# One base tile and three neighbour steps per chunk, in place of two base tiles and one step

## The chip, the cores and the metric

The kernel runs on one core of a Trainium2 chip. The metric is the device time of one execution in microseconds (us). Each kernel was run several times, in turn with the kernel before on the same chip. A run counts as slow when it lies over 1.5% above the fastest of the same kernel. Medians are over all runs of a kernel.

The engines are named as the profile names them: PE (TensorE matmul), PEld (its weight load), DVE (VectorE), ACT (ScalarE), POOL (GpSimd), SP (SyncE, which issues most of the DMAs here). A q behind a name is that engine's sequencer, which hands out its instructions. PSUM is the memory that the matmuls write.

## The reference, cut to what matters

Set attention with 32 inducing points over four batches of 12480 tokens, then a feed-forward layer on every token:

```python
# x: 4 x 12480 x 128, inducing: 32 x 128, w_in: 128 x 2048, w_out: 2048 x 128
h = mab(I, x)            # softmax over the tokens: 32 rows of 128 per batch
y = mab(x, h)            # softmax over the 32 rows: one row of 128 per token
u = y @ w_in
out = (u * clip(u + 3, 0, 6) / 6) @ w_out
```

## The kernel before

A batch is 25 chunks of up to 512 tokens. Four chunks are a group; six groups are full, the seventh has one short chunk of 192 tokens. While a batch's output is made, the next batch is loaded and aggregated (the `h` above), so the run has a start, three middle stages that do both, and a last stage that only makes output.

For the quadratic part of the feed-forward layer the kernel needs exponentials of sums of score rows: 4 tiles of 128 features per token. It does not compute them all with their own matmul. Two *base* tiles are made by a matmul and an exponential each. A *neighbour step* `d` is the exponential of a difference of score rows; it has only 32 rows, and is shared by four features each. Base times step, on DVE, gives two further tiles. The step of four chunks is made by four 32-column matmuls side by side (a *pack*; the four take 0.23 us together in the trace before), which leaves chunk j's 32 rows on partitions 32j to 32j+31 of `dk`. A DMA then spreads each row over four partitions of `d`.

```python
dpk: bufs=2   dp: bufs=4   tf: bufs=LEAD + 1   td: bufs=LEAD   osp: bufs=2   # buffers in SBUF
psF: bufs=5                                                                # PSUM banks, shared

def b_pack(b, g):                    # one per group of four chunks
    pp = psF.tile([P, 512], FP32, name="pp", tag="fb")
    for j in range(J):
        nc.tensor.matmul(pp[32 * j : 32 * j + 32, :w], lhsT=st["Wd"][:, :],
            rhs=st["xT"][:, t0 + j * w : t0 + (j + 1) * w], tile_position=(0, 32 * j))
    t = dpk.tile([P, 512], BF16, name="dk")
    nc.scalar.activation(t[: 32 * J, :w], pp[: 32 * J, :w], ACT.Exp, scale=scale)

def b_spread(b, c):                  # one per chunk, on the SP queue
    d = dp.tile([P, 512], BF16, name="d")
    nc.sync.dma_start(d[:, :w],
        st[("dk", g)][32 * j : 32 * j + 32, :w].unsqueeze(1).to_broadcast([32, 4, w]))

def b_base(b, c, k):                 # two per chunk, k = 0, 1
    nc.tensor.matmul(bp[:, :w], lhsT=st["W"][:, k]..., rhs=st["xT"][:, c0 : c0 + w])
    nc.scalar.activation(st[("x", c)][:, k, :w], bp[:, :w], ACT.Exp, scale=scale)

def b_prod(b, c):                    # one per chunk
    u = td.tile([P, 2, 512], BF16, name="TD")
    nc.vector.tensor_mul(u[:, :, :w], t[:, :, :w], d[:, :w].unsqueeze(1).to_broadcast([P, 2, w]))
    st[("T", c)] = [t[:, 0], u[:, 0], u[:, 1], t[:, 1]]
# ... 16 matmuls of 128 columns a chunk (b_quad) and one of 512 (b_lin) make its output `op`;
# DVE divides it into `os` (b_evac), and every four chunks 1 MB leaves on the SP queue

for t in range(total):               # cut: the work of the next batch goes in between
    b_evac(t - 1); b_spread(t + 4); b_prod(t + 1); b_base(t + 2, 0)
    b_lin(t); b_quad(t, 0); b_quad(t, 1); # b_pack of the group that begins at t + LEAD + 3
    b_base(t + 2, 1); b_quad(t, 2); b_quad(t, 3)
```

## Time and profile before

| | before |
|---|---|
| median of 3 runs | 324.52 us (322.81 to 328.84) |
| span of the profiled run | 319.7 us |
| PE, DVE, ACT busy | 94%, 75%, 72% |
| spread: size, from issue to landing | 128 KB, 4.1 us |

The share of busy time is read first, then by stage; the prediction below shows both. Here are the chain that ended last (by engine and by line), the largest output group and the row of the SP queue (packets, MB, share of the time of 16 DMA engines).

```profile
PE 86%; DVE 5%; ACT 3%; DMA 2%; issue 1%; POOL 0%; POOLq 0%
...
L692 PE MATMUL op<-Cq,TD 128*128 128x128 bf16 (+1 forms) x800 | 106.6, 220 | 0.4 <-DVE TD L668 0.4
...
q1 hardware_dynamic: 18160, 38.36, 37.3%
```

The chain is almost all PE. The output matmuls that take products waited 0.4 us for DVE in the whole run. The SP queue, which carries the spreads and the outputs, took little over a third of the DMA engines' time.

### The profile page before, as it was taken

To read this page: it belongs to the slowest core of one execution; us is meant where nothing else is said; L and a number is where in the kernel's file an instruction comes from. 1 tells how busy PE (TensorE), PEld (TensorE's weight loads), DVE (VectorE), ACT (ScalarE), POOL (GpSimd) and SP (SyncE) were. 2 spreads that over 40 slices of the span, in tenths; PEclk is the share of its full clock that TensorE was granted. 3 is DMA by queue.
4 is the path that set the end of the run, shared out by engine and by line. 5 is a ranking of instruction groups with operands and counts; after the bars stand their busy time and mean duration, and the time that the engine had idled before them with its cause. 6 is when DMAs were issued, how large, how long until landed. Compare 5 with 4: busy or idle time off the path is not lost.

```text
span 319.7 us, 9627 instructions
## 1 busy us (share of the span) xinstructions
PE 301.0 (94%) x3934; PEld 235.9 (74%) x3934; DVE 238.3 (75%) x542; ACT 229.6 (72%) x416; POOL 23.3 (7%) x59
## 2 busy tenths in 40 slices
PE   6788998999999998999999998999999999999991
PEld 2685766888767786888777786888777787777771
DVE  2678676787895776887796776978796777888873
ACT  2472778887679758887589758888489856777750
POOL 8150020111000000110100000100000000000000
PEclk9599998999999999999999999999999999999997
DMA  6999399599975256589984256461554355567643
GB/s 225 422 272 276 73 351 357 193 297 281 398 242 189 65 144 195 176 263 332 340 303 160 62 182 200 128 217 35 183 171 143 102 172 185 173 219 216 214 169 152
DMA packets 26481, 67.73 MB, mean 212 GB/s; under 512 B 5152, under 2 KB 19520, under 8 KB 20288
## 3 DMA queue, kind: packets, MB, share of 16 engines
q1 hardware_dynamic: 18160, 38.36, 37.3%
q0 software_dynamic: 8272, 28.71, 29.1%
q8 instruction: 32, 0.52, 0.7%
q14 instruction: 17, 0.14, 0.1%
HBM read 29.77 MB, written 25.56 MB: 173 GB/s over the span
## 4 chain that ended last, share of the span: by engine, by line
PE 86%; DVE 5%; ACT 3%; DMA 2%; issue 1%; POOL 0%; POOLq 0%
PE op L692 29%; PE bp L652 13%; PE hnd L282 8%; PE op L676 7%; PE pt L260 6%; PE cp L490 4%; PE dpm L470 4%; PE s L268 3%; PE pp L623 3%; DMA xr<-in_x_dram 2%; DVE xT L261 2%; PE sp L593 2%; PE ep L579 2%; PE lp L444 1%; DVE TD L668 1%
## 5 line engine op out<-in xcount | busy, mean ns | idle before, releaser
L659 ACT ACTIVATE TF<-bp 128x512 bf16<-128x512 f32 (+1 forms) x200 | 117.9, 600 | 36.0 <-PE rp L612 22.4
L692 PE MATMUL op<-Cq,TF 128*128 128x128 bf16 (+1 forms) x800 | 109.5, 223 | 0.0
L692 PE MATMUL op<-Cq,TD 128*128 128x128 bf16 (+1 forms) x800 | 106.6, 220 | 0.4 <-DVE TD L668 0.4
L708 DVE TENSOR_TENSOR os<-op,r_all 128x512 f32<-128x512 f32 (+1 forms) x100 | 68.4, 684 | 20.0 <-PE op L692 19.1
L692 PEld LDWEIGHTS <-TF 128*128 128x128 bf16 (+1 forms) x800 | 50.9, 98 | 33.8 <-issue 25.7
L652 PE MATMUL bp<-xT,W 128*128 128x512 bf16 (+1 forms) x200 | 75.3, 377 | 0.0
L668 DVE TENSOR_TENSOR TD<-TF,d 128x1024 bf16<-128x1024 bf16 (+1 forms) x100 | 67.0, 670 | 4.2 <-ACT TF L659 3.5
L692 PEld LDWEIGHTS <-TD 128*128 128x128 bf16 (+1 forms) x800 | 61.6, 98 | 0.7 <-DVE TD L668 0.5
L676 PE MATMUL op<-BD,nf 128*128 128x512 f32 (+1 forms) x100 | 53.6, 536 | 0.0
L251 ACT CAST xb<-xr 128x1024 bf16<-128x1024 f32 (+1 forms) x47 | 46.0, 1002 | 7.6 <-DMA xr<-in_x_dram 7.6
L481 ACT ACTIVATE sq<-dpm 128x512 bf16<-128x512 f32 x60 | 36.5, 644 | 5.6 <-PE dpm L470 3.7
L261 DVE COPY xT<-pt 128x1024 bf16<-128x1024 bf16 (+1 forms) x56 | 33.8, 618 | 8.6 <-PE pt L260 8.4
L613 DVE RECIPROCAL r_all<-rp 128x4 f32<-128x4 f32 (+1 forms) x100 | 17.9, 179 | 24.3 <-PE rp L612 23.7
L612 PE MATMUL rp<-one,nf 128*128 128x4 f32 (+1 forms) x100 | 34.3, 343 | 0.1
L260 PE MATMUL pt<-ident_b,xb 128*128 128x128 bf16 (+1 forms) x400 | 31.4, 225 | 2.1 <-DVE xb L251 1.6
L282 PE MATMUL hnd<-xr,a 128*32 128x128 f32 x384 | 32.2, 231 | 0.5 <-ACT a L274 0.5
L282 PEld LDWEIGHTS hnd<-xr,a 128*32 128x32 f32 x384 | 26.0, 113 | 2.7 <-issue 2.1
L260 PEld LDWEIGHTS <-xb 128*128 128x128 bf16 (+1 forms) x400 | 25.0, 101 | 4.0 <-DVE xb L251 1.7
L119 POOL DMA_DIRECT2D xr<-in_x_dram x25 | 13.5, 544 | 162.4 <-ACT TF L659 93.5
L490 PE MATMUL cp<-w_out_b,sq 128*128 128x128 bf16 x256 | 24.3, 220 | 0.4 <-ACT sq L481 0.4
L470 PE MATMUL dpm<-dH,w_in_b 128*128 128x512 bf16 x64 | 23.7, 381 | 0.8 <-DVE dH L400 0.5
L630 ACT ACTIVATE dk<-pp 128x512 bf16<-128x512 f32 (+1 forms) x28 | 15.8, 564 | 11.5 <-PE pp L623 10.5
(106 smaller groups left out, 344.3 us busy)
## 6 DMA issues: line engine op xcount, KB each, us to landing
out_dram<-os SPq DMA_DIRECT2D x24, 1024.0 KB, 4.2
xr<-in_x_dram POOLq DMA_DIRECT2D x23, 1024.0 KB, 7.8
d<-dk SPq DMA_DIRECT2D x96, 128.0 KB, 4.1
xr<-in_x_dram POOLq DMA_DIRECT2D x2, 512.0 KB, 4.6
w_in_r<-in_moe_w_in_dram POOLq DMA_DIRECT2D x1, 1024.0 KB, 10.1
w_out_r<-in_moe_w_out_dram POOLq DMA_DIRECT2D x1, 1024.0 KB, 14.4
w_in_b<-in_moe_w_in_dram POOLq DMA_DIRECT2D x1, 512.0 KB, 7.5
w_out_b<-in_moe_w_out_dram POOLq DMA_DIRECT2D x1, 512.0 KB, 12.3
```

Source lines behind the costliest of these rows:

```text
L251: eng(xb[:p, lo:hi, :], xs[(b, g)][:p, lo:hi, :].bitcast(FP32))
L260: nc.tensor.transpose(pt[:, (i - lo) * p : (i - lo + 1) * p], xb[:p, i, :], ident_b[:p, :p])
L261: nc.vector.tensor_copy(st["xT"][:, t0 + lo * p : t0 + hi * p], pt[:, : (hi - lo) * p])
L282: nc.tensor.matmul(st["hnd"][:M, :C], lhsT=a1[:p, i * M : (i + 1) * M], rhs=xs[(b, g)][:p, i, :], start=(g == 0 and i == 0), stop=(g == NG ...
L481: nc.scalar.activation(sq[:, :], dpm[:, :], ACT.Square)
L490: nc.tensor.matmul(st["cp"][:, k * C : (k + 1) * C], lhsT=sq[:, k * P : (k + 1) * P], rhs=w_out_b[:, jc, :], start=(jc == 0 and k == 0), s ...
L652: nc.tensor.matmul(bp[:, :w], lhsT=st["W"][:, k].rearrange("p m i -> p (m i)"), rhs=st["xT"][:, c0 : c0 + w],)
L659: nc.scalar.activation(st[("x", c)][:, k, :w], bp[:, :w], ACT.Exp, scale=scale)
L668: nc.vector.tensor_mul(u[:, :, :w], t[:, :, :w], d[:, :w].unsqueeze(1).to_broadcast([P, 2, w]))
L676: nc.tensor.matmul(op[:p, :], lhsT=st[("nf", g)][:, j * p : (j + 1) * p], rhs=st["BD"][:, :], start=True, stop=False, skip_group_check=True,)
L692: nc.tensor.matmul(op[:p, s * C : (s + 1) * C], lhsT=T[k][:, s * p : (s + 1) * p], rhs=st["Cq"][:, k, :], start=False, stop=(s == SL - 1 a ...
L708: nc.vector.tensor_mul(ot[:p, j * SL : (j + 1) * SL, :], op[:p, :].rearrange("p (s c) -> p s c", c=C), r_all[:p, b, c, :].unsqueeze(2).to_ ...
```

## The change

The intent: PE sets the end, and a base tile costs a full 512-column matmul per chunk (0.21 us), a pack about one such slot (0.22 to 0.23 us) per *four* chunks. So one base tile per chunk goes away and two more steps per group come in: four tiles are now base, base x d1, base x d2, base x d3. The three steps of a chunk lie next to each other in `dk`, and one DMA of 384 KB, in rows of 3 KB, spreads them. To make room in SBUF, outputs leave in halves of 512 KB, fewer `sq` buffers are kept, and one tile shares another's place.

```diff
-SQB = 12
+SQB = 8
-        osp = es.enter_context(tc.tile_pool(name="osp", bufs=2))
+        osp = es.enter_context(tc.tile_pool(name="osp", bufs=3))
@@ b_pack
+            t = dpk.tile([P, 3, 512], BF16, name="dk")
+            for k in range(3):
+                pp = psF.tile([P, 512], FP32, name="pp", tag="fb")
+                ...                              # the four matmuls, with st["Wd"][:, k]
+                nc.scalar.activation(t[: 32 * J, k, :w], pp[: 32 * J, :w], ACT.Exp, scale=scale)
@@ b_spread
-            d = dp.tile([P, 512], BF16, name="d")
-                st[("dk", g)][32 * j : 32 * j + 32, :w].unsqueeze(1).to_broadcast([32, 4, w]),
+            d = dp.tile([P, 3, 512], BF16, name="d")
+            src = st[("dk", g)][32 * j : 32 * j + 32]
+            if w == 512:
+                nc.sync.dma_start(
+                    d[:, :, :].rearrange("p k w -> p (k w)"),
+                    src.rearrange("m k w -> m (k w)").unsqueeze(1).to_broadcast([32, 4, 3 * w]),
+                )
+            else:                                # the short chunk: three small transfers
+                ...
@@ b_prod
-            u = td.tile([P, 2, 512], BF16, name="TD")
-            nc.vector.tensor_mul(u[:, :, :w], t[:, :, :w], d[:, :w].unsqueeze(1).to_broadcast([P, 2, w]))
-            st[("T", c)] = [t[:, 0], u[:, 0], u[:, 1], t[:, 1]]
+            u = td.tile([P, 3, 512], BF16, name="TD")
+            nc.vector.tensor_mul(u[:, :, :w], d[:, :, :w], t[:, :w].unsqueeze(1).to_broadcast([P, 3, w]))
+            st[("T", c)] = [t, u[:, 0], u[:, 1], u[:, 2]]
@@ main loop
-                b_base(fb_, fc, 0)
+                b_base(fb_, fc)
 ...
-            if feat:
-                b_base(fb_, fc, 1)
# cut: coefficients and weights that follow from the new features, outputs in halves, d32 under r6's name
```

More of the change, by code (lines that the diff above doesn't have):

```diff
@@ L128, in load_held @@
             seen = cst.tile([P, 1], BF16, name="seen")
-            nc.gpsimd.tensor_copy(seen[:, :], S[0][("d", c)][:, 0:1])
+            nc.gpsimd.tensor_copy(seen[:, :], S[0][("d", c)][:, 0, 0:1])
             for _ in range(n):
@@ L397, in c_HT @@
             st["dH"] = dH
-            nc.vector.tensor_sub(dH[:, 0], shifted(HT, 0, 1, 0), shifted(HT, 2, 0, 4))
-            nc.vector.tensor_sub(dH[:, 1], shifted(HT, 1, -1, 0), shifted(HT, 4, 0, 4))
-            W = coef.tile([P, 2, M, 4], BF16, name="W")
-            nc.vector.tensor_add(W[:, :], shifted(HT, 0, 0, 0), shifted(HT, 2, 2, 4))
-            Wd = coef.tile([P, M], BF16, name="Wd")
-            nc.vector.tensor_sub(Wd[:, :], HT[:, :, :].rearrange("p a m -> p (a m)")[:, 1 : M + 1], HT[:, 0])
+            nc.vector.tensor_sub(dH[:, 0], shifted(HT, 0, 1, 0), shifted(HT, 4, 0, 4))
+            nc.vector.tensor_sub(dH[:, 1], shifted(HT, 2, 1, 0), shifted(HT, 4, 0, 4))
+            W = coef.tile([P, M, 4], BF16, name="W")
+            nc.vector.tensor_add(W[:, :, :], shifted(HT, 0, 0, 0)[:, 0], shifted(HT, 4, 0, 4)[:, 0])
+            Wd = coef.tile([P, 3, M], BF16, name="Wd")
+            for k in range(3):
+                nc.vector.tensor_sub(
+                    Wd[:, k], HT[:, :, :].rearrange("p a m -> p (a m)")[:, k + 1 : k + 1 + M], HT[:, 0]
+                )
             st["W"], st["Wd"] = W, Wd
@@ L476, in c_sq @@
             if b == 0 and jb % 4 == 1:
-                d32 = cst.tile([P, 512], FP32, name="d32")
+                d32 = cst.tile([P, 512], FP32, name="r6")
                 nc.vector.tensor_copy(d32[:, :], dpm[:, :])
@@ L502, in c_tail @@
             cp = st["cp"]
-            nc.vector.tensor_scalar_mul(Cq[:, 0:3, :].rearrange("p k c -> p (k c)"), cp[:, : 3 * C], -1.0 / 6.0)
-            nc.vector.tensor_scalar_mul(Cq[:, 3, :], cp[:, 3 * C : 4 * C], half_of[:, 0:1])
+            nc.vector.tensor_scalar_mul(Cq[:, 1:4, :].rearrange("p k c -> p (k c)"), cp[:, C : 4 * C], -1.0 / 6.0)
+            nc.vector.tensor_scalar_mul(Cq[:, 0, :], cp[:, :C], half_of[:, 0:1])
             st["Cq"] = Cq
@@ L516, in c_units @@
                 us += [cs[jb - SQB], lambda jb=jb: (c_sq(b, jb), c_G(b, jb, jb + 1))]
-            us += ls[0:1] + cs[4:6] + ls[1:3] + cs[6:8] + ls[3:] + cs[8:]
+            n = FB - SQB
+            us += ls[0:1] + cs[n : n + 2] + ls[1:3] + cs[n + 2 : n + 4] + ls[3:] + cs[n + 4 :]
             return us + [lambda: c_tail(b)]
@@ L545, in c_first @@
             sq(8)
-            b_base(0, 0, 0)
-            b_base(0, 0, 1)
+            b_base(0, 0)
             cs(5)
@@ L558, in c_first @@
             cs(8)
-            b_base(0, 1, 0)
+            b_base(0, 1)
             b_r(0, 0)
@@ L563, in c_first @@
                 cs(jb - 3)
-            b_base(0, 1, 1)
             cs(13, 14, 15)
@@ L620, in b_pack @@
             w = SL * p
-            pp = psF.tile([P, 512], FP32, name="pp", tag="fb")
-            for j in range(J):
-                nc.tensor.matmul(
-                    pp[32 * j : 32 * j + 32, :w],
-                    lhsT=st["Wd"][:, :],
-                    rhs=st["xT"][:, t0 + j * w : t0 + (j + 1) * w],
-                    tile_position=(0, 32 * j),
-                )
-            t = dpk.tile([P, 512], BF16, name="dk")
-            nc.scalar.activation(t[: 32 * J, :w], pp[: 32 * J, :w], ACT.Exp, scale=scale)
+            t = dpk.tile([P, 3, 512], BF16, name="dk")
+            for k in range(3):
+                pp = psF.tile([P, 512], FP32, name="pp", tag="fb")
+                for j in range(J):
+                    nc.tensor.matmul(
+                        pp[32 * j : 32 * j + 32, :w],
+                        lhsT=st["Wd"][:, k],
+                        rhs=st["xT"][:, t0 + j * w : t0 + (j + 1) * w],
+                        tile_position=(0, 32 * j),
+                    )
+                nc.scalar.activation(t[: 32 * J, k, :w], pp[: 32 * J, :w], ACT.Exp, scale=scale)
             st[("dk", g)] = t
@@ L637, in b_spread, with b_base @@
             w = SL * groups[g][1]
-            d = dp.tile([P, 512], BF16, name="d")
-            nc.sync.dma_start(
-                d[:, :w],
-                st[("dk", g)][32 * j : 32 * j + 32, :w].unsqueeze(1).to_broadcast([32, 4, w]),
-            )
+            d = dp.tile([P, 3, 512], BF16, name="d")
[4 more added lines that the diff above has]
+                    src.rearrange("m k w -> m (k w)").unsqueeze(1).to_broadcast([32, 4, 3 * w]),
+                )
+            else:
+                for k in range(3):
+                    nc.sync.dma_start(
+                        d[:, k, :w], src[:, k, :w].unsqueeze(1).to_broadcast([32, 4, w])
+                    )
             st[("d", c)] = d
-        def b_base(b, c, k):
+        def b_base(b, c):
             g, j = chunks[c]
@@ L653, in b_base @@
                 bp[:, :w],
-                lhsT=st["W"][:, k].rearrange("p m i -> p (m i)"),
+                lhsT=st["W"][:, :, :].rearrange("p m i -> p (m i)"),
                 rhs=st["xT"][:, c0 : c0 + w],
             )
-            if k == 0:
-                st[("x", c)] = tf.tile([P, 2, 512], BF16, name="TF")
-            nc.scalar.activation(st[("x", c)][:, k, :w], bp[:, :w], ACT.Exp, scale=scale)
+            t = tf.tile([P, 512], BF16, name="TF")
+            nc.scalar.activation(t[:, :w], bp[:, :w], ACT.Exp, scale=scale)
+            st[("x", c)] = t
         def b_prod(b, c):
@@ L690, in b_quad @@
             T = st[("T", c)]
-            for k in (0, 3, 1, 2):
+            for k in range(4):
                 nc.tensor.matmul(
@@ L696, in b_quad @@
                     start=False,
-                    stop=(s == SL - 1 and k == 2),
+                    stop=(s == SL - 1 and k == 3),
                     skip_group_check=True,
@@ L704, in b_evac @@
             st = S[b]
-            if j == 0:
-                st["os"] = osp.tile([P, TG, C], FP32, name="os")
+            HG = min(n, TG // 2)
+            lo = j * SL % HG
+            if lo == 0:
+                st["os"] = osp.tile([P, TG // 2, C], FP32, name="os")
             ot = st["os"]
             nc.vector.tensor_mul(
-                ot[:p, j * SL : (j + 1) * SL, :],
+                ot[:p, lo : lo + SL, :],
                 op[:p, :].rearrange("p (s c) -> p s c", c=C),
@@ L712, in b_evac @@
             )
-            if (j + 1) * SL == n:
+            if lo + SL == HG:
+                i0 = j * SL - lo
                 r0 = b * N + t0
                 nc.sync.dma_start(
-                    out[r0 : r0 + p * n, :].rearrange("(p i) c -> p i c", i=n), ot[:p, :n, :]
+                    out[r0 : r0 + p * n, :].rearrange("(p i) c -> p i c", i=n)[:, i0 : i0 + HG, :],
+                    ot[:p, :HG, :],
                 )
```

## The prediction

> **What bounds the kernel now.** The page comes first, then the same sums by stage: one batch of 25 chunks per stage. I cut it at 48, 122, 195.5 and 268.5 us: the first product goes out at 47.9 us, and a batch's last output, the small one of 96 KB, leaves a little after each later cut.
>
> ```profile
> PE 301.0 (94%) x3934; PEld 235.9 (74%) x3934; DVE 238.3 (75%) x542; ACT 229.6 (72%) x416; POOL 23.3 (7%) x59
> core 0: us, PE busy (x) PEld busy (x) DVE busy (x) ACT busy (x) POOL busy (x), PEclk, DMA share, GB/s
> 0.00:48.00 48.00, 40.48 (x485) 29.52 (x486) 31.31 (x67) 26.40 (x47) 14.85 (x43) 0.93 0.97 270
> 48.00:122.00 74.00, 72.45 (x957) 57.25 (x955) 54.82 (x123) 57.47 (x105) 3.73 (x7) 0.98 0.72 242
> 122.00:195.50 73.50, 72.19 (x982) 57.77 (x979) 56.81 (x129) 57.93 (x106) 3.73 (x7) 1.00 0.67 220
> 195.50:268.50 73.00, 71.69 (x977) 57.48 (x976) 56.28 (x128) 56.64 (x105) 1.03 (x2) 1.00 0.48 148
> 268.50:316.00 47.50, 44.18 (x542) 33.90 (x540) 39.04 (x100) 31.12 (x57) 0.00 (x0) 1.00 0.63 205
> ```
>
> PE is busy for all but 1.3 to 1.6 us of each of the three middle stages, where a batch's output is made while the next is aggregated; the last stage (output alone) takes 1.9 us a chunk. PE's busy span is modelled, so this is support, not proof. The chain of waits agrees: it gives PE 86%, DVE 5%, ACT 3%, DMA 2%. DVE and ACT have slack on average. DMA has slack too, least in the stage that still loads x (0.72) and in the short last one (0.63).
>
> The groups that the change touches:
>
> ```profile
> L659 ACT ACTIVATE TF<-bp 128x512 bf16<-128x512 f32 (+1 forms) x200 | 117.9, 600 | 36.0 <-PE rp L612 22.4
> L652 PE MATMUL bp<-xT,W 128*128 128x512 bf16 (+1 forms) x200 | 75.3, 377 | 0.0
> L668 DVE TENSOR_TENSOR TD<-TF,d 128x1024 bf16<-128x1024 bf16 (+1 forms) x100 | 67.0, 670 | 4.2 <-ACT TF L659 3.5
> L630 ACT ACTIVATE dk<-pp 128x512 bf16<-128x512 f32 (+1 forms) x28 | 15.8, 564 | 11.5 <-PE pp L623 10.5
> d<-dk SPq DMA_DIRECT2D x96, 128.0 KB, 4.1
> ```
>
> A mean of 377 ns is latency; what a matmul costs is the step between starts, which the timeline has (last stage):
>
> ```profile
> 288.18 0.28 PE L692 MATMUL op<-Cq,TD 128*128 128x128 bf16 x2
> 288.29 0.38 PE L652 MATMUL bp<-xT,W 128*128 128x512 bf16 x1
> 288.32 0.58 PE L676 MATMUL op<-BD,nf 128*128 128x512 f32 x1
> ...
> 289.29 0.40 PE L623 MATMUL pp<-xT,Wd 128*32 128x512 bf16 x4
> 289.52 0.39 PE L579 MATMUL ep<-xT,HTb 128*32 128x512 bf16 x4
> ```
>
> One base matmul takes 0.21 us: where base plus the small reciprocal matmul stand together the next weights load 0.30 us later, and the latter alone costs some 0.09. A pack of four 32-column matmuls takes 0.23 us in all (289.29 to 289.52), so the four run side by side.
>
> What carries my doubt is the transfer of d. Three stretches in which one sort of transfer runs nearly alone: four spreads of 128 KB, one output of 1 MB, one spread of 48 KB.
>
> ```profile
> 35.30:38.50 3.20, 3.20 (x31) 2.36 (x29) 2.91 (x5) 2.13 (x5) 0.00 (x0) 1.00 0.72 164
> 307.40:309.90 2.50, 2.50 (x36) 2.14 (x35) 2.28 (x7) 1.51 (x4) 0.00 (x0) 1.00 1.04 419
> 309.90:310.50 0.60, 0.60 (x9) 0.44 (x8) 0.58 (x3) 0.32 (x1) 0.00 (x0) 1.00 0.35 82
> ```
>
> The last two columns are DMA share and GB/s. Share times time times 16 engines over the packets (128 a transfer) gives the time of one packet: 0.72 x 3.2 x 16 / 512 = 72 ns for 1 KB; 1.04 x 2.5 x 16 / 128 = 325 ns for 8 KB of output; 0.35 x 0.6 x 16 / 128 = 26 ns for 384 B. A spread moves 14 to 15 GB/s per engine at either size, an output 25. So the spread's cost grows with bytes, not with packets, and longer rows should not make it cheaper.
>
> [...] Outputs and spreads share the SP queue here, so a spread behind an output waits for it. [...] 1024 bf16 elements take 683 ns and the 512-element product from PSUM 685. [...]
>
> **The change, part by part.**
>
> PE. Removed: one base per chunk, 4 x 0.21 = 0.84 us a group. Added: two more packs a group, 2 x 0.22 = 0.44. Net 0.40 us a group, over 24 full groups 9.6 us, all on PE, which sets the end now. The sixteen output matmuls of a chunk stay. Stage by stage this is 2.4 us: 74, 73.5, 73 and 47.5 become 71.6, 71.1, 70.6 and 45.1 if nothing else steps in.
>
> ACT. Removed: 4 x 0.60 a group; added: 2 x 0.60; 1.2 us a group, 29 us in all. ACT is off the path, so this is worth only fewer late features (DVE waited 3.5 us for them). But three exponentials now come in a row at a pack, and PE fills banks faster (0.22) than ACT empties them (0.55): of the five shared banks three are then held by packs. I expect up to 0.2 us of PE waiting in some groups, some 1 to 3 us in all.
>
> DVE. The product grows from 1024 to 1536 elements: [...]0.27 us more, 683 to 950 ns; 26 us over 96 chunks. In a middle stage DVE goes from 56 to 63 of 71 us, hidden. In the last it goes from 39.0 to some 45: level with PE, so little is won there. Back to back its instructions start about 0.57 us apart where they last 0.68, so it can still keep up. The coefficient step trades a half-size W for three short differences: nothing.
>
> DMA. A spread grows from 128 to 384 KB. At 72 ns per KB and 8 packets an engine, 0.58 us of all engines becomes 1.73; 1.15 more for each full chunk. Outputs keep their bytes in halves of 512 KB, which lets a spread in sooner. Load by stage, share times length plus the new part: 53 + 28 = 81 us in 48 to 122 (against 71.6 for PE); 49 + 28 = 77 in the next (71.1); 35 + 28 = 63 in the third (70.6); 30 + 24 = 54 in the last (45.1). Share reaches 1.04 to 1.05 when saturated, so the floors are near 78, 74, 60 and 52 us. Then stage one loses 4 us, stage two 0.5, stage three gains 2.4, and the last loses 5, plus a tail of a few chunks after the last spread, say 1. Start: the first four spreads need 1.5 MB before the held loads of x may go, and two exponentials come before them; 1 to 2 us.
>
> Sum on this path: +4 + 0.5 - 2.4 + 6 + 1.5 + 1 (banks) = +10.6, or 335 from 324.5.
>
> **The rivals.**
>
> One: PE stays the bound. For it: [...]x comes by another queue[...]; d has four buffers. Then the whole 9.6 us less 2 to 3 for banks and start: 317 to 318. Against: four spreads queued behind an output at 302 to 305 us again took near 3 us, at a share below 1.
>
> Two: partial overlap. The middle stages gain 1 to 2 us each, the last loses 2, the start 1.5: 320 to 326.
>
> Three: DVE becomes the bound in the last stage, at 1.75 to 1.8 us a chunk. It would only take back that stage's gain: 319 to 320. [...]
>
> Four: under steady load [...]a spread slows further; nothing in this trace loads spreads deeply enough to tell. Then 350 or more.
>
> **Range and chances.** DMA as the bound in two stages at 335 (weight 0.4), partial overlap at 323 (0.3), PE bound at 317 (0.22), worse DMA at 350 (0.08): mean 328.8. I take 329, with 315 to 345 as the range. Faster than 318 needs nearly the whole PE gain: 0.23. Slower than 331 is the DMA path and the worse one without their mildest part: 0.42. Within 2%: 0.35.
>
> **What would show it.** PE step: the base group halves to 100, the pack group goes from 96 to 288 matmuls, PE busy time falls by some 10 us. DVE step: product near 950 ns. ACT: L659's group at about 60 us. DMA step: each spread 384 KB, landing well above 4.1 us (7 or more), share near 1 in the last stage; the product then waits for "DMA d<-dk", and PE for the product, where the kernel before has no such rows. The last stage is the test: longer than 47.5 us if DMA binds, near 45 to 46 if not. If a 384 KB spread costs clearly under 1.7 us of engine time, or waits for d are absent, the DMA step is wrong and the time is near 317. If the start grows by over 3 us, the gate on the held loads was undervalued.

Passages that no trace or run shows are cut from the prediction, and from three of the expectations below (a_rows64, a_step4, b_packs); each cut is marked. No term of the forecast's sum is among them: it still comes to +10.6 us, or 335 from 324.5. Four things that stand there have their numbers in the traces. The 0.27 us of the longer product is an estimate: a product of 384 elements takes 348 ns and one of 1024 takes 683, so 512 more come to 0.27 us at that rate. A spread waits behind an output: one issued at 299.25 us, behind an output of 1 MB, sent its first packet at 302.23, when the output's last ones went (302.46); with nothing before it in the queue, one issued at 34.19 sent its first at 35.49. That halves let a spread in sooner shows in b_house, where spreads land in 3.1 us and not in 4.1. The share was 0.99 to 1.11 in the single microseconds from 3 to 15 us, and 1.05 in that from 5 to 6.

## The result, and the profile after

| | before | after |
|---|---|---|
| median of 4 runs each, same rounds | 324.96 us | 390.03 us |
| range | 322.81 to 328.84 | 389.56 to 395.42 (the last one slow) |
| span, granted clock of the profiled run | 319.7 us, 0.978 | 388.6 us, 0.926 |

The ratio is 1.202 (95% interval 1.194 to 1.211). All ratios here are the mean time of one kernel's fast runs over that of the other's fast runs of the same rounds, so not quite the ratio of the medians. Where a ratio is turned into microseconds below, it is multiplied by 325 us. The kernel became 20% slower, where 329 was predicted and 345 was the upper end.

The page of the kernel after, with the chain that ended last, the groups that the change touched (busy us, mean ns | idle before, what ended most of it), the SP queue and the spreads:

```profile
PE 320.3 (82%) x4034; PEld 247.9 (64%) x4034; DVE 260.8 (67%) x550; ACT 204.5 (53%) x372; POOL 23.3 (6%) x59
...
q1 hardware_dynamic: 22768, 63.92, 63.6%
...
PE 39%; DMA 33%; DVE 12%; issue 10%; SPq 2%; POOL 2%; ACT 1%; DVEq 0%; ACTq 0%; POOLq 0%
DMA d<-dk 30%; PE op L702 15%; DVE TD L678 4%; DMA xr<-in_x_dram 3%; PE op L686 3%; PE pt L260 3%; PE bp L662 3%; PE cp L493 3%; PE dpm L473 3%; PE hnd L282 2%; PE pp L627 2%; DVE os L720 2%; DVE xT L261 2%; PE s L268 1%; PE rp L614 1%
...
L702 PE MATMUL op<-Cq,TD 128*128 128x128 bf16 (+1 forms) x1200 | 133.7, 230 | 23.4 <-DVE TD L678 22.8
L678 DVE TENSOR_TENSOR TD<-d,TF 128x1536 bf16<-128x1536 bf16 (+1 forms) x100 | 93.1, 931 | 50.1 <-DMA d<-dk 43.9
...
L668 ACT ACTIVATE TF<-bp 128x512 bf16<-128x512 f32 (+1 forms) x100 | 59.3, 593 | 76.5 <-PE bp L662 65.4
...
L633 ACT ACTIVATE dk<-pp 128x512 bf16<-128x512 f32 (+1 forms) x84 | 40.8, 559 | 29.3 <-DMA d<-dk 16.3
...
d<-dk SPq DMA_DIRECT2D x96, 384.0 KB, 7.3
```

Read from the bottom: a spread takes 7.3 us to land; the product waits 43.9 us for spreads; PE waits 22.8 us for products, where it waited 0.4 before; and the spread, which the page's chain before did not list, is now 30% of it. The exponential of the pack also waits for spreads: `dk` has two buffers, and the packs of a third group may not overwrite those of the first before the last spread has read them.

By stage (start, three middle stages, last stage; each later cut is about 1 us before the batch's small output leaves, as near as may be to where the prediction's table has it):

```profile
core 0: us, PE busy (x) PEld busy (x) DVE busy (x) ACT busy (x) POOL busy (x), PEclk, DMA share, GB/s
0.00:49.00 49.00, 41.18 (x500) 29.43 (x501) 32.11 (x69) 26.95 (x48) 14.82 (x43) 0.97 0.94 243
49.00:140.00 91.00, 75.94 (x980) 60.17 (x980) 59.95 (x125) 51.89 (x93) 3.73 (x7) 0.91 0.93 290
140.00:231.50 91.50, 76.40 (x1009) 60.51 (x1006) 62.21 (x131) 52.15 (x96) 3.72 (x7) 0.94 0.88 248
231.50:313.00 81.50, 74.25 (x1004) 59.43 (x1003) 62.04 (x131) 51.05 (x94) 1.03 (x2) 0.96 0.84 209
313.00:384.50 71.50, 52.51 (x551) 38.35 (x549) 44.44 (x99) 22.49 (x44) 0.00 (x0) 0.88 0.88 213
```

Against 74, 73.5, 73 and 47.5 us before, the four stages take 91, 91.5, 81.5 and 71.5: 17, 18, 8.5 and 24 us more. PE is idle for 7 to 19 us of each, and the DMA share is 0.84 to 0.93. That is below the 1.04 that the prediction read as saturated, but the 1.04 was that of one output. Spreads don't reach it: the first four of this kernel, nearly alone, took 8.4 us at a share of 0.86. In the steady part of the last stage (317 to 372 us) the queue is at 92%, so there the DMA engines have little left. In the middle stages neither they nor PE are full, and the chain passes from one to the other (PE 39%, DMA 33%).

Three products of the last stage, and the chain that ended last through the same stretch (start, us, what):

```profile
340.58 0.96 DVE L678 TENSOR_TENSOR TD<-d,TF 128x1536 bf16<-128x1536 bf16 x1 [2.01 <-DMA d<-dk]
...
343.19 0.96 DVE L678 TENSOR_TENSOR TD<-d,TF 128x1536 bf16<-128x1536 bf16 x1 [0.37 <-DMA d<-dk]
...
346.13 0.96 DVE L678 TENSOR_TENSOR TD<-d,TF 128x1536 bf16<-128x1536 bf16 x1 [1.31 <-DMA d<-dk]
```

```profile
339.07 6.97 DMA d<-dk
346.04 0.03 issue
346.07 0.02 DVEq L678
346.09 0.04 issue
346.13 0.33 DVE TD L678
346.46 0.33 issue
346.79 7.64 DMA d<-dk
```

The brackets give the idle time of DVE just before a product and what ended it. Of the last batch's 25 products, 17 wait for their spread (20.8 us in all) and two for the exponential behind `dk` (4.4 us). In the chain one spread follows another, with under a microsecond of anything else between.

The `dk` wait at its worst, in a middle stage:

```profile
216.90 1.57 ACT L633 ACTIVATE dk<-pp 128x512 bf16<-128x512 f32 x3 [7.48 <-DMA d<-dk]
217.54 0.58 PE L473 MATMUL dpm<-dH,w_in_b 128*128 128x512 bf16 x1 [7.29 <-ACT dk L633]
```

ACT does nothing else in these 7.5 us, since its next instruction is the one that waits. By the program the three packs occupy three of the five shared PSUM banks meanwhile, and PE stands still behind them for 7.3 us. This happened where a batch ends: the short last group needs a `dk` of its own, so the packs of three groups fall within five chunks.

### The profile page after: what moved, and what is told of

It is laid out like the page before. It is cut to its first block, busy times and chain, and to the rows that moved or that the text cites. A ratio compares the mean times of both kernels' runs of the same rounds, so it can differ in the third digit from the quotient of the medians.

```text
span 388.6 us, 9833 instructions
## 1 busy us (share of the span) xinstructions
PE 320.3 (82%) x4034; PEld 247.9 (64%) x4034; DVE 260.8 (67%) x550; ACT 204.5 (53%) x372; POOL 23.3 (6%) x59
## 4 chain that ended last, share of the span: by engine, by line
PE 39%; DMA 33%; DVE 12%; issue 10%; SPq 2%; POOL 2%; ACT 1%; DVEq 0%; ACTq 0%; POOLq 0%
DMA d<-dk 30%; PE op L702 15%; DVE TD L678 4%; DMA xr<-in_x_dram 3%; PE op L686 3%; PE pt L260 3%; PE bp L662 3%; PE cp L493 3%; PE dpm L473 3%; PE hnd L282 2%; PE pp L627 2%; DVE os L720 2%; DVE xT L261 2%; PE s L268 1%; PE rp L614 1%
## 5 line engine op out<-in xcount | busy, mean ns | idle before, releaser
L702 PE MATMUL op<-Cq,TD 128*128 128x128 bf16 (+1 forms) x1200 | 133.7, 230 | 23.4 <-DVE TD L678 22.8
L678 DVE TENSOR_TENSOR TD<-d,TF 128x1536 bf16<-128x1536 bf16 (+1 forms) x100 | 93.1, 931 | 50.1 <-DMA d<-dk 43.9
L702 PEld LDWEIGHTS <-TD 128*128 128x128 bf16 (+1 forms) x1200 | 89.7, 104 | 26.4 <-DVE TD L678 26.3
L668 ACT ACTIVATE TF<-bp 128x512 bf16<-128x512 f32 (+1 forms) x100 | 59.3, 593 | 76.5 <-PE bp L662 65.4
L702 PE MATMUL op<-Cq,TF 128*128 128x128 bf16 (+1 forms) x400 | 94.3, 236 | 0.0
L702 PEld LDWEIGHTS <-TF 128*128 128x128 bf16 (+1 forms) x400 | 40.3, 101 | 30.8 <-issue 27.7
L633 ACT ACTIVATE dk<-pp 128x512 bf16<-128x512 f32 (+1 forms) x84 | 40.8, 559 | 29.3 <-DMA d<-dk 16.3
L662 PE MATMUL bp<-xT,W 128*128 128x512 bf16 (+1 forms) x100 | 39.9, 399 | 0.1
L614 PE MATMUL rp<-one,nf 128*128 128x4 f32 (+1 forms) x100 | 26.4, 264 | 7.1 <-DVE xT L261 4.2
L614 PEld LDWEIGHTS rp<-one,nf 128*128 128x128 f32 (+1 forms) x100 | 20.3, 203 | 11.6 <-DVE xT L261 4.5
```

What stands on the lines that cost most here:

```text
L614: nc.tensor.matmul(rp[:p, :SL], lhsT=nf[:, j * p : (j + 1) * p], rhs=one4[:, :])
L633: nc.scalar.activation(t[: 32 * J, k, :w], pp[: 32 * J, :w], ACT.Exp, scale=scale)
L662: nc.tensor.matmul(bp[:, :w], lhsT=st["W"][:, :, :].rearrange("p m i -> p (m i)"), rhs=st["xT"][:, c0 : c0 + w],)
L668: nc.scalar.activation(t[:, :w], bp[:, :w], ACT.Exp, scale=scale)
L678: nc.vector.tensor_mul(u[:, :, :w], d[:, :, :w], t[:, :w].unsqueeze(1).to_broadcast([P, 3, w]))
L702: nc.tensor.matmul(op[:p, s * C : (s + 1) * C], lhsT=T[k][:, s * p : (s + 1) * p], rhs=st["Cq"][:, k, :], start=False, stop=(s == SL - 1 a ...
```

## The experiments

Two theories stood at the outset. *Transfer*: the time comes from the spreads, because they are too many bytes, or because they read 32 neighbouring partitions. *Rest*: it comes from the other parts (the longer product, three packs and exponentials in a row, fewer buffers). Kernels whose names begin with `a_` start from the kernel after, `b_` ones from the kernel before. They ran on several chips, each next to the kernel before, so across runs it is the ratios that are compared, and not the medians. Several give a wrong result, and each is named where it comes. The comparison with the reference doesn't tell one neighbour step from another, so it is no proof for these.

### Only a third of the bytes (a_third, wrong)

The spread takes the first step alone, 128 KB as before; the product uses it three times. Packs, exponentials and product length stay as after.

```diff
-            (the 384 KB transfer)
+            nc.sync.dma_start(d[:, 0, :w],
+                st[("dk", g)][32 * j : 32 * j + 32, 0, :w].unsqueeze(1).to_broadcast([32, 4, w]))
-            nc.vector.tensor_mul(u[:, :, :w], d[:, :, :w], ...)
+            nc.vector.tensor_mul(u[:, :, :w], d[:, 0:1, :w].to_broadcast([P, 3, w]), ...)
```

> The changed kernel with a third of the spread's bytes: the transfer carries only the first step (128 KB, 1 KB rows) and the product takes it three times. Wrong result on purpose; packs, exponentials, products and output halves stay as they are. Supply theory (the spread's transfer sets the time): the PE gain of the prediction appears, 316 to 323 us, no long waits for d. Structure theory (the three packs in a row, the longer product, the banks cost the time): stays above 360 us. Housekeeping theory (split outputs, fewer sq buffers): stays above 360 us as well.

Measured: 328.65 us, ratio 1.017 (1.009 to 1.025). The time lies just outside the nearer of the two ranges (316 to 323). The transfer is nearly the whole loss: 1.202 less 1.017 is 0.185, or 60 us. But without it the change still doesn't win anything, which the next groups take up.

### All bytes, other source partitions (a_rows128, a_rows64, a_step4; all wrong)

All move 384 KB per spread into the same `d` in rows of 3 KB. They differ in which partitions are read: all 128 once; 0 to 63, each twice; 32 that lie four apart, each four times, as after.

```diff
-                    src.rearrange("m k w -> m (k w)").unsqueeze(1).to_broadcast([32, 4, 3 * w]),
+  a_rows128:       st[("dk", g)][:, :, :].rearrange("m k w -> m (k w)"),
+  a_rows64:        st[("dk", g)][0:64].rearrange("m k w -> m (k w)").unsqueeze(1).to_broadcast([64, 2, 3 * w]),
+  a_step4:         st[("dk", g)][:, :, :].rearrange("(m f) k w -> m f (k w)", f=4)[:, j]
+                       .unsqueeze(1).to_broadcast([32, 4, 3 * w]),
```

> The changed kernel with the same 384 KB and the same 128 rows of 3 KB a spread, but each row read from its own partition (all 128 rows of the packed tile) in place of 32 rows read four times. Wrong result on purpose. If the source's 32 rows are what makes the spread slow: the transfer runs near the output's 25 GB/s an engine, 0.95 us of DMA a spread, and the time falls to 318 to 335 us. If SBUF to SBUF is slow as such, or bytes alone decide: 375 to 395 us.

> The changed kernel with the source rows taken from partitions 0 to 63, each read twice, in place of 32 rows read four times; same 128 rows of 3 KB. Wrong result on purpose. [...] 375 to 400 us, nothing won. If it comes from reading the same row several times: about half of the loss goes, 345 to 365 us.

> The changed kernel with the 32 source rows of a spread taken four partitions apart (j, j+4, ... j+124) in place of 32 neighbours; each is still read four times, same rows of 3 KB, same bytes. Wrong result on purpose. [...] 326 to 336 us, as with 128 rows. If reading one row four times is the cause: 385 to 395 us. The run with 64 rows left this open[...].

The two ranges without their condition are those for no gain from 64 rows (a_rows64) and for the place of the rows as the cause (a_step4).

Measured: a_rows128 330.22 us, 1.024 (1.015 to 1.032); a_rows64 369.00 us, 1.138 (1.131 to 1.146); a_step4 332.51 us, 1.030 (1.021 to 1.038). a_rows64 fell between its two ranges and decides neither way; the other two are inside their first.

a_step4 settles it. It reads as many rows, each as often, with the same length and bytes as the kernel after; only the place of the 32 rows differs, and that is worth 1.202 - 1.030, or 56 us. The waits go with it; these are a_step4's product and spread, to be held against those of the kernel after (43.9 us of waits, 7.3 us to land):

```profile
L678 DVE TENSOR_TENSOR TD<-d,TF 128x1536 bf16<-128x1536 bf16 (+1 forms) x100 | 93.0, 930 | 7.1 <-DMA d<-dk 7.1
...
d<-dk SPq DMA_DIRECT2D x96, 384.0 KB, 4.3
```

Why the place of the rows decides is not shown by any run here. The first four spreads of the run, which have the queue nearly to themselves, show the difference directly. Here is the throughput (GB/s) in 40 slices of 34.5 to 46.0 us, 0.29 us each, for the kernel after, a_step4 and a_rows64 in turn:

```profile
GB/s 0 0 0 0 0 139 128 64 128 53 139 150 289 289 182 171 118 203 182 363 274 192 310 278 224 267 192 171 171 182 160 192 203 75 11 0 0 0 28 0
```

```profile
GB/s 0 0 0 0 0 385 353 406 342 406 363 395 364 406 406 374 424 385 374 64 11 21 21 0 0 0 0 0 0 0 0 228 114 256 228 399 427 427 399 456
```

```profile
GB/s 0 0 0 0 85 214 192 203 182 235 224 193 182 214 182 214 246 171 214 203 192 221 246 160 225 225 214 182 214 203 182 86 0 0 0 0 0 28 0 0
```

From the first packet to the last, the same 1.57 MB take 8.4 us (186 GB/s) from 32 neighbours. From rows four apart they take 5.1 us (305 GB/s), of which some 4 us are at about 390 GB/s and the rest is a thin tail. Partitions 0 to 63 take 8.0 us (197), little less than 32 neighbours. Even so a_rows64 gained 21 us on the kernel after; its burst doesn't explain that.

What a spread costs in the steady state is read from the DMA packets. For the kernel after, 317 to 372 us:

```profile
q1 hardware_dynamic: 3895, 11.82, 92.2%
...
d<-dk SPq DMA_DIRECT2D x18, 384.0 KB, 7.4
out_dram<-os SPq DMA_DIRECT2D x10, 512.0 KB, 7.5
```

That is 0.922 x 55 = 50.7 us of all 16 engines. The packed trace holds every packet with its size and time, which `prof` only sums up, so it can be split: packets of 3 KB (or 1 KB) belong to spreads, those of 4 KB (8 KB in the kernel before) to outputs. The fastest and the slowest tenth are the times that a tenth of the packets doesn't exceed, or exceeds. A spread of 384 KB has 128 packets of 3 KB on 16 engines, so its cost in time of all engines is 128 times the mean over 16; for 1 KB packets, 384 times.

| kernel, stretch (us) | spread packets: mean ns | fastest, slowest tenth | 384 KB of spreads, us of all engines | output packets: mean ns |
|---|---|---|---|---|
| after, 317 to 372 | 3 KB: 263 | 121, 500 | 2.10 | 172 |
| a_rows64, 300 to 350 | 3 KB: 226 | 121, 289 | 1.81 | 177 |
| a_step4, 270 to 320 | 3 KB: 128 | 121, 142 | 1.02 | 164 |
| a_rows128, 281 to 315 | 3 KB: 125 | 121, 131 | 1.00 | 163 |
| a_rows1k (below), 310 to 358 | 1 KB: 71 | 46, 139 | 1.69 | 165 |
| before, 277 to 306 | 1 KB: 70 | 46, 140 | 1.68 (0.56 for its 128 KB) | 327 (8 KB) |

A fast packet of 3 KB takes 121 ns in all four kernels with such rows. What differs is how many are held up (take longer than that), and for how long (the slowest tenth from 131 to 500 ns); the outputs in the same queue hardly change (163 to 177 ns). What holds the packets up, the trace does not name. The steady state also shows where a_rows64 won: there a packet took 226 ns against 263, while in the first burst it took 233 against 226. Why is open.

### The two ends of the change alone (b_house, b_bytes; both right)

b_house is the kernel before with only the side edits: outputs in halves, three output buffers of half size, 8 `sq` buffers, the shared tile.

```diff
-SQB = 12
+SQB = 8
-        osp = es.enter_context(tc.tile_pool(name="osp", bufs=2))
+        osp = es.enter_context(tc.tile_pool(name="osp", bufs=3))
-                d32 = cst.tile([P, 512], FP32, name="d32")
+                d32 = cst.tile([P, 512], FP32, name="r6")
 # and b_evac with outputs in halves, as in the change
```

> The kernel before with only the side edits of the change: outputs in halves of 512 KB from three half-size buffers, 8 sq buffers instead of 12, and the shared name of the first stage's copy. Supply theory: within 2% of before, 322 to 330 us. Housekeeping theory: most of the loss is here, above 350 us.

b_bytes adds to it only the bytes: each spread takes 3 KB rows, of which the last 2 KB are zeros that nobody uses; two base tiles, one pack and a product of 1024 stay. (SQB is 7 here, for room.)

```diff
+        dkc = [...]                # two constant tiles [P, 3, 512], zeroed once
-            t = dpk.tile([P, 512], BF16, name="dk")
+            t = dkc[g % 2]
-            nc.scalar.activation(t[: 32 * J, :w], ...)
+            nc.scalar.activation(t[: 32 * J, 0, :w], ...)
+            # b_spread as after; the product takes d[:, 0]
```

> The kernel of the run before this one (7 sq buffers) with each spread three times as large: the packed tile has two further columns of zeros, the transfer moves all 3 KB rows from 32 partitions, the product reads only the first 1 KB. Nothing else of the change; right result. Supply theory: 370 to 400 us, close to the changed kernel, as PE has more to do but DMA the same. Structure theory: no more than 335 us.

Measured: b_house 322.92 us, 0.998 (0.989 to 1.006); b_bytes 393.49 us, 1.219 (1.210 to 1.229). The side edits cost nothing. The bytes alone, in a kernel whose PE, ACT and DVE work is that of before, cost as much as the whole change (1.219 against 1.202). The product of b_bytes, with its 1024 elements, waits as that of the kernel after does, and the chain agrees:

```profile
DMA 40%; PE 34%; issue 10%; DVE 9%; ACT 3%; SPq 1%; POOL 1%; DVEq 0%; ACTq 0%; POOLq 0%
...
L680 DVE TENSOR_TENSOR TD<-TF,d 128x1024 bf16<-128x1024 bf16 (+1 forms) x100 | 67.2, 672 | 76.5 <-DMA d<-dkc 48.4
```

### What the long transfer is made of (a_rows1k, a_dk3; both right)

a_rows1k sends the same data as three transfers of 1 KB rows; a_dk3 gives `dk` a third buffer (and takes two from `sq`, for room).

```diff
# a_rows1k
-            if w == 512:
+            if False:                    # three transfers of 128 KB each
# a_dk3
-SQB = 8
+SQB = 6
-        dpk = es.enter_context(tc.tile_pool(name="dpk", bufs=2))
+        dpk = es.enter_context(tc.tile_pool(name="dpk", bufs=3))
```

> The changed kernel with each spread as three transfers of 1 KB rows in place of one of 3 KB rows; same bytes, same source partitions, right result. In the last stage a 3 KB spread took 2.3 us of all engines where three times the old one would take 1.8. If long rows are the dearer ones: the time falls to 355 to 370 us. If the rate is lost because the queue is full, whatever the rows: 385 to 400 us.

> The changed kernel with three buffers for the packed tile in place of two (6 sq buffers to make room); right result. ScalarE waited 16 us for spreads before it could overwrite that tile, and PE 13 us behind it. If these waits are a cost of their own: 370 to 382 us. If the transfer alone sets the pace and these waits only show it: 385 to 393 us.

Measured: a_rows1k 376.59 us, 1.164 (1.150 to 1.178); a_dk3 377.45 us, 1.161 (1.148 to 1.175). The profiled run of a_dk3 was a slow one, so nothing is read from that profile; the ratio has its three fast runs. a_dk3 is inside its first range; a_rows1k fell between its two.

Each takes 13 us off the kernel after. So the wait for `dk` is worth about 13 us of the 56, and the length of the rows about 13. a_rows1k also makes three transfers of one, which no run separates from the length of the rows, and a_dk3 has two `sq` buffers fewer. They weren't tried together, so the two need not add up. The steady stretch of a_rows1k, 310 to 358 us:

```profile
q1 hardware_dynamic: 8792, 11.55, 87.2%
...
d<-dk SPq DMA_DIRECT2D x53, 128.0 KB, 3.3
out_dram<-os SPq DMA_DIRECT2D x9, 512.0 KB, 3.9
```

The queue is less full than in the kernel after (87.2% against 92.2%) though it moves as much in a shorter time (11.55 MB in 48 us against 11.82 in 55). By the packets (table above) 384 KB cost 1.69 us in 1 KB rows against 2.10 in 3 KB rows, where the expectation had 1.8 against 2.3. 1.69 is about what the prediction took, three times the 0.58 us of a 1 KB-row spread. The held-up packets are dearer in proportion when rows are long: 500 ns for 121, against 139 for 46. Why is not shown by any run here.

### Where the gain on PE went (b_onebase, b_packs, a_packs, b_dve, a_thin)

With the transfer cheap (a_third) the kernel should have won 9.6 us on PE, and lost 5.5. These runs take the parts one by one. b_onebase is b_house without the second base matmul and exponential (wrong); b_packs is b_house with three packs and three exponentials a group, of which one is used (right). a_packs is a_third with its three packs in three successive chunks rather than in a row (wrong, like a_third). b_dve is b_house with a product of 1536 elements; a_thin is a_third with one of 1024 (both wrong).

```diff
# b_onebase
-                b_base(fb_, fc, 1)
-            nc.vector.tensor_mul(u[:, :, :w], t[:, :, :w], ...)
+            nc.vector.tensor_mul(u[:, :, :w], t[:, 0:1, :w].to_broadcast([P, 2, w]), ...)
+            st[("T", c)] = [t[:, 0], u[:, 0], u[:, 1], t[:, 0]]
# b_packs
+            for k in range(3):          # pp, four matmuls, exponential; same Wd each time
+            (the spread takes step 0)
# a_packs
-   ahead.setdefault(t - LEAD - 3, []).append(lambda b=b, g=g: (b_pack(b, g), b_e(b, g)))
+   ahead.setdefault(t - LEAD - 5, []).append(lambda b=b, g=g: b_pack(b, g, (0,)))
+   ahead.setdefault(t - LEAD - 4, []).append(lambda b=b, g=g: b_pack(b, g, (1,)))
+   ahead.setdefault(t - LEAD - 3, []).append(lambda b=b, g=g: (b_pack(b, g, (2,)), b_e(b, g)))
# b_dve
+            u = td.tile([P, 3, 512], BF16, name="TD")
+            nc.vector.tensor_mul(u[:, :, :w], t[:, 0:1, :w].to_broadcast([P, 3, w]), d broadcast to 3)
# a_thin
+            nc.vector.tensor_mul(u[:, 0:2, :w], d[:, 0:1, :w].to_broadcast([P, 2, w]), t broadcast to 2)
```

> The kernel before with the side edits and without its second base matmul and exponential; the product keeps its length, the first base tile stands in for the second (wrong result on purpose). The prediction's sum puts 0.21 us of PE a chunk on the path: 20 us less, 300 to 305 us. If PE is only one of several that set the pace, less than half of that: 312 to 320 us.

> The kernel before with the side edits and with three packs and three exponentials a group in place of one (the two more are not used; right result). Prediction: 0.44 us of PE a group plus 1 to 3 us for banks, together 11 to 14 us: 334 to 337 us. If the packs cost more than their matmuls ([...]waits for banks): over 340 us.

> The run with a third of the spread's bytes, with the three packs of a group put in three successive chunks in place of one after the other. Same work. If the burst of three packs (banks filled faster than ScalarE empties them) swallows the gain: 318 to 324 us, against 328.7. If the longer product does: 326 to 330.

> The kernel before with the side edits (322.9 us) and only its product made as long as the changed kernel's: 1536 elements (wrong result on purpose), transfers and packs as before. Rough sum: 0.27 us more for each of 96 chunks, 26 us of DVE time. If DVE has slack, as the prediction took it in the three middle stages: under 327 us. If the product is on the path: 330 to 345 us.

> The run with a third of the spread's bytes, with a product of 1024 elements in place of 1536 (two of the three steps; wrong result on purpose). If the longer product on DVE is what swallows the PE gain when the transfer is cheap: 316 to 321 us, against 328.7. If it is the three packs in a row: 326 to 329.

| run | median | ratio | 95% |
|---|---|---|---|
| b_house | 322.92 | 0.998 | 0.989 to 1.006 |
| b_onebase | 307.34 | 0.952 | 0.944 to 0.960 |
| b_packs | 338.45 | 1.044 | 1.037 to 1.051 |
| b_dve | 322.94 | 0.995 | 0.988 to 1.001 |
| a_thin | 326.37 | 0.997 | 0.987 to 1.006 |
| a_third | 328.65 | 1.017 | 1.009 to 1.025 |
| a_packs | 344.74 | 1.058 | 1.049 to 1.066 |

Against b_house, the base matmul and its exponential are worth 0.046, or 15 us; the two added packs and exponentials cost 0.046, or 15 us. Their difference is nothing, to within some 5 us (the intervals above are about 0.008 to either side), and a_thin, which has both, stands at 0.997. That is where the gain on PE went. Both runs fell between the two ranges for them. The packs themselves cost on PE what was foreseen (b_packs, last stage; start, us, and how many):

```profile
292.76 0.83 PE L626 MATMUL pp<-xT,Wd 128*32 128x512 bf16 x12
293.42 0.39 PE L580 MATMUL ep<-xT,HTb 128*32 128x512 bf16 x4
```

Three packs take 0.66 us from start to the next start, 0.44 more than one: 24 x 0.44 = 10.6 us. The other 4 us lie in the middle stages. By the distance of the small outputs (129.23, 209.62 and 287.73 us against 126.50, 200.97 and 273.97 in b_house) the second and the third are 5.9 and 5.1 us longer, where the added packs on PE account for some 3 (seven groups of 0.44). Waits around the exponentials of the packs fit this ("ACT dk L632 5%" stands in the chain of b_packs), but no run separates them.

a_packs was a miss: spreading the packs out was expected to relieve the banks (in a row, a pack fills one every 0.22 us, and an exponential takes 0.56) and win, and it lost 0.04 against a_third. A lone pack of it, and its neighbours:

```profile
314.39 0.33 PE L696 MATMUL op<-Cq,TD 128*128 128x128 bf16 x3
314.65 0.40 PE L629 MATMUL pp<-xT,Wd 128*32 128x512 bf16 x4
314.98 0.27 PE L614 MATMUL rp<-one,nf 128*128 128x4 f32 x1
```

The lone pack takes 0.33 us to the next start, where one within a row takes 0.22. Before it, three `op` matmuls take 0.26 us to the next start, where three of the same form take 0.17 before another of 128 columns (314.16 to 314.33). So a lone pack loses about 0.09 us before it and 0.11 after it. Three packs in a row lose as much only once, with the `ep` matmuls of the same form behind them: in b_packs two `op` matmuls take 0.20 us in front of the row instead of 0.12, and the four `ep` matmuls take 0.32 to the next start. What causes the loss is not shown. PE was busy for 310.9 us against 300.8 in a_third. As an estimate from these lines, 0.1 to 0.2 us for each of 48 more lone packs is 5 to 10 of the 13 us. ACT also waited for lone packs (31.3 us in 41 waits).

The longer product costs nothing in the old design (b_dve less b_house is -0.003) and 0.020, or 6.6 us, in the new one (a_third less a_thin). The second figure is the weaker: the two ran on different chips, their intervals only just miss each other, and a_thin's fast runs (mean 324.2 us) lie outside both of its ranges. The profiled runs are 3.3 us apart, 2.3 of them in the last stage: from the third batch's last division into `os` to the last of all it takes 45.6 us in a_third and 43.3 in a_thin, against 44.8 in b_house. A product takes 928 ns in b_dve and in a_third; a_third's last stage shows why it can cost there (start, us, with brackets only where DVE was idle):

```profile
301.85 0.66 DVE L713 TENSOR_TENSOR os<-op,r_all 128x512 f32<-128x512 f32 x1
302.43 0.95 DVE L671 TENSOR_TENSOR TD<-d,TF 128x1536 bf16<-128x1536 bf16 x1
303.30 0.17 DVE L615 RECIPROCAL r_all<-rp 128x4 f32<-128x4 f32 x1
303.39 0.66 DVE L713 TENSOR_TENSOR os<-op,r_all 128x512 f32<-128x512 f32 x1
303.97 0.95 DVE L671 TENSOR_TENSOR TD<-d,TF 128x1536 bf16<-128x1536 bf16 x1
```

No gap: over 273 to 327 us DVE is busy for 44.5 us and PE for 45.7, so each can delay the other. In b_dve PE still has the second base to do in each chunk, and DVE has room.

### What the sum is, and what stays open

From the kernel before to the kernel after, in shares of the time before: base removed and packs added, about 0 (a_thin 0.997); longer product, some +0.02 (a_third 1.017, weakly shown); three times the bytes from 128 rows or from 32 rows four apart, +0.006 to +0.013 (a_rows128, a_step4; their intervals overlap that of a_third); the same bytes from 32 neighbouring rows, +0.173 to +0.179 (after, 1.202). Of the last, some 0.04 are the wait for `dk` and some 0.04 the long rows.

Open are why long rows cost more than short ones, why the place of the rows decides, why 64 partitions won 21 us although their first burst was hardly faster (197 against 186 GB/s), and which wait makes the packs dearer than their matmuls. Open is also the clock's part: the granted clock fell where there were long waits (0.926 in the kernel after, 0.940 in b_bytes, 0.986 in a_step4), and PE was busy for 320.3 us in the kernel after against 301.1 in a_step4, which does the same work. No run holds the clock and changes the waits. No run points to a right kernel that beats both: the only one clearly faster, b_onebase, leaves out features, and the right b_house is the same as before. Even with a spread as small as before, the new design came to 1.017, and to 0.997 with a product of the old length.

## Why the prediction was wrong

The spread's transfer does set the time, as the path with the largest weight had it. What failed is the step from the load of the DMA engines to time; the load itself was only somewhat too small.

*The floors: the step that failed.* The prediction added up the DMA load of a stage, divided it by a share ("1.04 to 1.05 when saturated") and took the larger of that and PE's work as the stage's length. The measured load is the packets' time in each stage of the table above, and agrees with its share times length:

| stage | load predicted, measured (us) | floor predicted | share reached | length |
|---|---|---|---|---|
| first middle | 81, 84 | 78 | 0.93 | 91 |
| second middle | 77, 80 | 74 | 0.88 | 91.5 |
| third middle | 63, 68.5 | 60 (PE: 70.6) | 0.84 | 81.5 |
| last | 54, 62.7 | 52 | 0.88 | 71.5 |

In all, 275 us of length became 335.5. With the measured loads the same method gives 81, 77, 70.6 and 60, or 289 us. So some 14 of the missing 61 us are load, and 47 are the method: the DMA engines didn't reach that share, PE wasn't full either, and the idle time of the one didn't hide behind the work of the other. The 1.04 that it shows is that of a single output. The prediction's own stretch of four spreads nearly alone shows 0.72, and under its first rival it noted near 3 us for four spreads "at a share below 1". "Stage three gains 2.4" became a loss of 8.5.

*DMA step: a mis-sized term.* "0.58 us of all engines becomes 1.73" measured 1.64, 1.72, 1.95 and 2.09 us by stage (the 3 KB packets of the trace), so it held while x was loaded beside it and was a sixth too small in the last stage. The prediction inferred from 48 KB, 128 KB and output transfers that "the spread's cost grows with bytes, not with packets", and had only seen spreads of 1 KB rows or less; 1.73 holds for 1 KB rows (1.69 in a_rows1k). Its mean of 72 ns for a 1 KB packet was right but hid that a fast one takes 46 ns and the slowest tenth 140: packets were held up already. It gave the partitions that a spread reads no term; a_step4 shows that the place of the rows decides (1.02 against 2.10 us of all engines).

*The wait for `dk`.* It isn't in the prediction, which counted four `d` buffers in favour of PE and did not look at the two of `dk`. Its price is about 13 us (a_dk3), a part of the 47 above. In the kernel before spreads landed in 4.1 us; the change trebled what must be read from a `dk` before it is free.

*PE step: "Net 0.40 us a group, over 24 full groups 9.6 us".* About zero. The removed base was worth 15 us and not the 20 of 4 x 0.21 x 24, and the packs cost 15 and not 10.6 (with "1 to 3" for banks, near). "PE busy time falls by some 10 us" was wrong too: 320.3 against 301.0 us, at a clock of 0.926 instead of 0.978 and with matmul means up from 220 to 230 ns; and at 0.986, in a_step4, it was still 301.1.

*DVE step.* Right: 931 ns for 950, hidden before the last stage and level with PE in it. "Little is won there" was mild: some 3 to 7 us lost over the whole run, weakly shown and only where the transfer was cheap.

*ACT step.* The base group halved to 59.3 us, as predicted. *Start.* The first product came at 48.5 us for 47.9, less than the 1 to 2 us given. *Signs to look for*: waits for "DMA d<-dk", PE waiting for the product, landing at 7.3 us, and a last stage well over 47.5 all came.

*Rivals and range.* One, two and three are out, though a reason of the first fits ("x comes by another queue"): a spread cost least, 1.64 us, where x was loaded beside it. Four, "under steady load" a spread slows further, was right about the slowing (226 ns a packet in the first burst, 263 in the steady state). It stood at a weight of 0.08 and with 350 us, against 390. The prediction said of it that "nothing in this trace loads spreads deeply enough to tell". That was an argument for a wider range upwards, not for a low weight.

## What to carry to other kernels

Before a DMA inside SBUF is made larger, ask which partitions it reads: the same bytes from 32 rows four apart instead of side by side cost 1.02 instead of 2.10 us of all engines here, and decided 56 of 390 us. Take the share at which a queue counts as full from the sort of transfer that will fill it: an output's was 1.04, that of these spreads 0.86 to 0.92. When a transfer moves from slack to near its bound, follow every buffer that it holds, the source as well as the destination: here a source tile that freed late stopped ACT for 7.5 us, and PE behind it for 7.3. Price an exchange of one piece of work for another by running each half alone, as what looked like 20 us against 11 was 15 against 15.
